# Linear attention and two MLPs: k and v on 128 partitions, earlier output operands, longer attention distances in the plan

## The chip, the cores and the metric

One NeuronCore of a Trainium2 chip runs the whole program. The metric is the device time of one execution in microseconds, given as the median of three runs. TensorE is PE in the profile, VectorE is DVE, ScalarE is ACT, GpSimd is POOL, and SP is the queue that issues nearly every DMA.

## The reference

The sizes: q, k and v are [8, 8, 576, 64] (batch, head, token, feature), and the result of attention, written as rows x[4608, 512], goes through two MLPs.

```python
q_s = exp(q - max(q, -1));  q_s = q_s / (sum(q_s, -1) + 1e-9)
k_s = exp(k - max(k, 2));   k_s = k_s / (sum(k_s, 2) + 1e-9)   # over the 576 tokens
kv = einsum('bhsd,bhse->bhde', k_s, v)
x = einsum('bhsd,bhde->bhse', q_s, kv)      # then rows (b, s), columns (h, d)
r = maximum(x @ w_in, 0);  x = (r * r) @ w_out              # w_in 512x2048
g = x @ w_gate;  out = (g * sigmoid(g) * (x @ w_val)) @ w_out2   # w_gate 512x1536
```

## The kernel before

Each float32 matmul is done as three products of a high part and a low part (`mm3`); `split` and `parts` make the parts with a cast on ACT and a subtraction on DVE. The 4608 rows are 9 blocks of 512. Blocks 0 to 2 go through the first MLP directly. Blocks 3 to 8 go through it as three pairs, and all blocks go through the second MLP as pairs, in seven products of quarter matrices instead of eight (`four`, `quarters`; the products come in the order "1", "5", "6", "2", "7", "3", "4").

**The order of the work.** The first block, to about 120 us, is an order written out by hand (`FIRST_BLOCK`). From there to the end of the gated half of the second MLP's first pair, `Plan.run` writes the order of every engine: it is a list scheduler that knows no times but those given in the source. Each unit is a generator whose `step` names an engine, a duration, what it needs, which buffers it takes and frees, and `land` and `wait`: with `wait=True` the unit's next step starts no earlier than the end plus `land`. Of the steps of one engine that could start within 0.3 us, the one with the lowest rank goes first. A step behind one of another engine is placed 1.7 us after its end where that was PE (0.4 us in the main stream of matmuls), 1.0 us where it was SP, and 0.2 us after the others. After the plan, Python's own order holds for SP, and the other engines are ordered by the framework.

**Attention in the plan.** `kv_unit` does two heads (`hp`): it loads k (`load_k`), starts `v_unit` (`load_v`), takes the maximum over tokens on DVE, transposes it on PE, reduces it on DVE, spreads it by a second transpose, subtracts on DVE, exponentiates on ACT, and `kv_sums` multiplies with v and a column of ones on PE. Tokens lie on 96 partitions with 6 tokens each, so a sum is 6 chunks for two heads. There are 32 such units: 4 at the start and 4 later in the hand-made order (`kv_steps`), 24 in the plan, 13 to 20 us apart.

**Operands of the first MLP's second product.** `out_part` has 24 operands besides those of product "1"; each is a `chunk`: a cast on ACT (L1182) and a subtraction on DVE (L1184) into one of 4 `uo` buffers. They have rank 1. At ranks below are `p5` (0.1) and `post` (0.2), which take results out of PSUM (L1242, L1258, L1272), and `sums` (0.5).

**The next x.** `second_x(1)` holds the operands of blocks 2 and 3 for the second MLP. Its first half is loaded by `after.load(0)` (four DMAs, L972) when the plan has ended; `between()` in `out_stage` splits it (L101, L102) between the products of the first pair's output.

Of the kernel before, what the change touches and what calls it, by code (L numbers as in the profile page):

```python
# [8 lines left out]
F32 = mybir.dt.float32  # L9
# [3 lines left out]
ALU = mybir.AluOpType  # L13
# [4 lines left out]
P = 128  # L18
# [4 lines left out]
def tile_linear_attention_two_mlps(  # L23
# [252 lines left out]
    def step(engine, d, needs=(), take=(), free=(), names=(), land=0.0, wait=False):  # L276
        return engine, d, needs, take, free, names, land, wait
# [286 lines left out]
    vt1 = att.tile([CK, 800], F32, name="vt")[:, 0:2 * NC * (D + 1)]  # L564
    vt1 = vt1.rearrange("p (h c d) -> p h c d", h=2, c=NC)
    kts, qs, qT, xT = {}, {}, {}, {}

    def load_k(b, hp, t=None):
        if t is None:
            t = kp.tile([CK, 2, NC, D], F32, name="kt", tag="kt")  # L570
        nc.sync.dma_start(t, k[b, 2 * hp:2 * hp + 2].rearrange("h (p c) d -> p h c d", c=NC))
        return t

    def load_v(b, hp, t=None):
        if t is None:
            t = vt1
        for h in range(2):
            nc.sync.dma_start(
                t[:, h, :, 0:D], v[b, 2 * hp + h].rearrange("(p c) d -> p c d", c=NC)
            )  # L580
        return t

    def load_kv(b, hp):
        kt = vt = None
        if hp % 2:
            kt, vt = (
                raws.tile([P, T], w_in.dtype, name="wraw", tag=f"raw{n}").bitcast(F32) for n in range(2)
            )
            kt = kt[:CK, 0:2 * NC * D].rearrange("p (h c d) -> p h c d", h=2, c=NC)
            vt = vt[:CK, 0:2 * NC * (D + 1)].rearrange("p (h c d) -> p h c d", h=2, c=NC)  # L590
            nc.gpsimd.memset(vt[:, :, :, D:D + 1], 1.0)
        kts[b, hp] = load_k(b, hp, kt), load_v(b, hp, vt)

# [45 lines left out]

    def kv_unit(j, i, hp):  # L640
        me = ("kv", j)
        yield step("SP", 0.5, [("kt.", j - 1)] + ([("x", 1, 3)] if j == 1 else []), [("kt", j)], (), [("kt.", j)], LAND_A, True)
        kt = None
        if hp % 2:
            kt = qtp.tile([P, 2, T], F32, name="kt", tag="qT1").rearrange("p a n -> p (a n)")
            kt = kt[:CK, 0:2 * NC * D].rearrange("p (h c d) -> p h c d", h=2, c=NC)
        kt = load_k(i, hp, kt)
        plan.unit(v_unit(j, i, hp), 2)
        yield step("DVE", 0.66)
        m3 = sp.tile([CK, 2, NC // 2, D], F32, name="m3", tag="m3", bufs=1)  # L650
        m1 = sp.tile([CK, 2, D], F32, name="m1", tag="m1")
# [3 lines left out]
        nc.vector.tensor_tensor(m1, m1, m3[:, :, 2], op=ALU.max)  # L655
# [5 lines left out]
        nc.vector.tensor_reduce(mx, pt[:, 0:CK], axis=AX.X, op=ALU.max)  # L661
        yield step("PE", 0.17)
        top = pt[:CK, P:2 * P]
        nc.tensor.transpose(top, mx.to_broadcast([P, CK]), ident)
        yield step("DVE", 0.95, (), (), [("pa", me)])
        nc.vector.tensor_tensor(
            kt, kt,
            top.rearrange("p (h d) -> p h d", h=2).unsqueeze(2).to_broadcast([CK, 2, NC, D]),
            op=ALU.subtract,
        )  # L670
        yield step("ACT", 0.84)
        nc.scalar.activation(kt, kt, AF.Exp)
        me = ("pk", j)
        yield step("PE", 1.0, [("vt.", j)], [("pa", me)], [("kt", j), ("vt", j)])
# [14 lines left out]

    def v_unit(j, i, hp):  # L690
        yield step("SP", 1.0, (), [("vt", j)], (), [("vt.", j)], LAND_A)
        load_v(i, hp)

    def q_unit(j, i, hp):
# [494 lines left out]
    def out_part(k, p, half, ops):  # L1189
# [294 lines left out]
    with tc.manual_schedule(engines={mybir.EngineType.SP}):  # L1484
# [41 lines left out]
        def kv_steps(b, hp):  # L1526
            if b:
                load_kv(b, hp)
                yield
            kt, vt = kts.pop((b, hp))  # L1530
            m3 = sp.tile([CK, 2, NC // 2, D], F32, name="m3", tag="m3", bufs=1)
            m = sp.tile([CK, 2, D], F32, name="m1", tag="m1")
            nc.vector.tensor_tensor(m3, kt[:, :, 0:3], kt[:, :, 3:6], op=ALU.max)
            yield
            nc.vector.tensor_tensor(m, m3[:, :, 0], m3[:, :, 1], op=ALU.max)
            yield
            nc.vector.tensor_tensor(m, m, m3[:, :, 2], op=ALU.max)
            yield
            pt = ps_a.tile([P, T], F32, name="pa", tag="pa")
            nc.tensor.transpose(pt[:, 0:CK], m.rearrange("p h d -> p (h d)"), ident[:CK, :CK])  # L1540
            yield
            mx = col.tile([P, 1], F32, name="mx", tag="mx")
            nc.vector.tensor_reduce(mx, pt[:, 0:CK], axis=AX.X, op=ALU.max)
            yield
            top = pt[:CK, P:2 * P]
            nc.tensor.transpose(top, mx.to_broadcast([P, CK]), ident)
            yield
            nc.vector.tensor_tensor(
                kt, kt,
                top.rearrange("p (h d) -> p h d", h=2).unsqueeze(2).to_broadcast([CK, 2, NC, D]),  # L1550
                op=ALU.subtract,
            )
            yield
# [172 lines left out]
        with tc.manual_schedule(engines=engines):  # L1726
# [102 lines left out]
```

## Time and profile before

| | us |
|---|---|
| median of 3 runs (1642.78 to 1643.26) | 1642.86 |
| the profiled execution | 1641.65 |
| its span, first to last instruction | 1639.8 |
| PE busy | 1602.0 |
| DVE busy | 1153.8 |
| ACT busy | 920.1 |

The span is the trace's; 1.85 us of the execution lie around it. An engine's busy time counts its instructions, overlapped ones once; what is left of the span is idle.

### The profile page before, as it was taken

Reading aid. Unit: us, or ns where it says so; the run is one execution under the profiler, and the core shown is the slowest. Engines: PE = TensorE matmul, PEld = TensorE weight load, DVE = VectorE, ACT = ScalarE, POOL = GpSimd, SP = SyncE. Lnnn points to the kernel's source line nnn. Section 1 sums busy time; section 2 is a strip of 40 time slices with the busy share of each in tenths; the row PEclk is TensorE's granted clock in tenths of the full one; section 3 lists DMA queues with packets and bytes.
Section 4 is the critical chain, followed back from the end, with each engine's and each line's share of the span. In section 5 each row is a group of like instructions: output and inputs, shape, how many; then the busy total and the mean of one; then the engine's idle time right before and its main releaser. Section 6 shows DMA issues by size and latency. Waiting matters only on the chain.

```text
span 1639.8 us, 23959 instructions
## 1 busy us (share of the span) xinstructions
PE 1602.0 (98%) x8114; PEld 1323.4 (81%) x8114; DVE 1153.8 (70%) x1857; ACT 920.1 (56%) x1561; POOL 376.9 (23%) x368
## 2 busy tenths in 40 slices
PE   7999999999999999999999999999999999999998
PEld 4777777878878888788878878888888888888898
DVE  8876776668978786888687778345844585447646
ACT  7775656668676776686755445334633463335334
POOL 4874554212221313021211200022001110210020
PEclk9999999999999999999999999999999999999999
DMA  9967999979998999899988987767686768667897
GB/s 300 282 208 235 306 307 302 300 237 291 270 283 255 290 327 330 302 348 322 349 288 298 307 293 235 231 192 219 219 243 193 220 210 253 194 204 210 264 385 257
DMA packets 280202, 440.97 MB, mean 269 GB/s; under 512 B 126864, under 2 KB 167824, under 8 KB 280080
## 3 DMA queue, kind: packets, MB, share of 16 engines
q1 hardware_dynamic: 279536, 439.30, 83.9%
q8 instruction: 65, 1.06, 0.3%
q14 instruction: 57, 0.47, 0.1%
q10 hardware_dynamic: 544, 0.13, 0.0%
HBM read 342.36 MB, written 96.99 MB: 268 GB/s over the span
## 4 chain that ended last, share of the span: by engine, by line
PE 81%; DVE 5%; DMA 5%; SPq 1%; ACT 1%; issue 1%; POOL 0%; DVEq 0%; POOLq 0%; ACTq 0%
PE ps L107 71%; PE acc L107 4%; PE ph L107 4%; DMA kt<-in_k_dram 2%; PE pa L617 1%; PE pa L107 1%; DVE uo L1184 1%; PE pa L734 1%; DMA w1d_out<-wbits 1%; DMA x<-x2d 0%; DVE st L1242 0%; DMA qs<-in_q_dram 0%; DVE u L1170 0%; DVE u L1168 0%; SPq L320 0%
## 5 line engine op out<-in xcount | busy, mean ns | idle before, releaser
L107 PE MATMUL ps<-w,wu 128*128 128x512 f32 (+1 forms) x3444 | 738.2, 375 | 1.2 <-ACT w L291 0.9
L107 PEld LDWEIGHTS ps<-w,wu 128*128 128x128 f32 x3444 | 610.3, 188 | 117.1 <-ACT w L291 1.4
L107 PE MATMUL ps<-uo,wu 128*128 128x512 f32 (+1 forms) x2172 | 475.5, 379 | 4.5 <-DVE uo L1184 2.7
L107 PEld LDWEIGHTS ps<-uo,wu 128*128 128x128 f32 x2172 | 390.2, 189 | 83.3 <-DVE uo L1184 5.5
L328 POOL TENSOR_TENSOR wsum<-wsum 128x256 f32<-128x256 f32 x124 | 112.4, 907 | 292.6 <-DVE wsum L404 130.9
L101 ACT CAST uo<-u 128x512 fp32r<-128x512 f32 (+1 forms) x204 | 116.4, 577 | 105.3 <-PE ps L107 42.6
L1436 POOL TENSOR_TENSOR u<-u 128x512 f32<-128x512 f32 (+1 forms) x24 | 27.6, 1152 | 577.6 <-DVE u L1432 577.6
L1431 DVE TENSOR_TENSOR u<-u,ps 128x512 f32<-128x512 f32 (+1 forms) x48 | 29.7, 620 | 174.5 <-ACT u L1430 174.5
L107 PE MATMUL ph<-xT,w 128*128 128x512 f32 x576 | 148.8, 399 | 2.1 <-ACT xT L771 0.7
L102 DVE TENSOR_TENSOR uo<-u,uo 128x512 fp32r<-128x512 f32 (+1 forms) x204 | 127.9, 645 | 31.0 <-ACT uo L101 30.7
L107 PE MATMUL acc<-g,w 128*128 128x512 f32 x576 | 145.0, 396 | 0.8 <-DVE g L1657 0.8
L1184 DVE TENSOR_TENSOR uo<-u,uo 128x512 fp32r<-128x512 f32 x168 | 116.4, 719 | 25.3 <-ACT uo L1182 25.1
L107 PEld LDWEIGHTS ph<-xT,w 128*128 128x128 f32 x576 | 105.1, 188 | 26.6 <-ACT xT L291 1.0
L107 PEld LDWEIGHTS acc<-g,w 128*128 128x128 f32 x576 | 105.6, 188 | 24.5 <-DVE g L1657 1.2
L1386 ACT COPY ps<-ps 128x512 f32<-128x512 f32 x102 | 58.1, 570 | 114.6 <-PE ps L107 113.4
L1182 ACT CAST uo<-u 128x512 fp32r<-128x512 f32 x168 | 100.0, 620 | 35.3 <-PE ps L107 34.3
L293 DVE TENSOR_TENSOR wst<-wsum,wst 128x512 fp32r<-128x512 f32 (+1 forms) x80 | 61.4, 770 | 21.2 <-ACT wst L291 18.9
L1086 ACT COPY ps<-ps 128x1024 f32<-128x1024 f32 x48 | 47.9, 998 | 50.0 <-PE ps L107 37.5
L714 POOL TENSOR_TENSOR qs<-qs,qr 128x512 f32<-128x512 f32 x28 | 32.1, 1147 | 124.9 <-DVE qr L712 94.1
L291 ACT CAST wst<-wsum 128x512 fp32r<-128x512 f32 (+1 forms) x80 | 46.8, 587 | 24.7 <-DVE wsum L404 12.0
L1138 ACT ACTIVATE u<-u 128x1024 f32<-128x1024 f32 x48 | 50.9, 1061 | 1.5
L293 DVE TENSOR_TENSOR g<-r,g 128x512 fp32r<-128x512 f32 x32 | 23.6, 739 | 38.9 <-ACT g L291 35.9
(216 smaller groups left out, 1891.5 us busy)
## 6 DMA issues: line engine op xcount, KB each, us to landing
wu<-gvd SPq DMA_DIRECT2D x210, 512.0 KB, 4.5
wu<-od SPq DMA_DIRECT2D x105, 512.0 KB, 4.4
wu<-hd SPq DMA_DIRECT2D x77, 512.0 KB, 6.1
wu<-ad SPq DMA_DIRECT2D x76, 512.0 KB, 5.2
gvd<-wst SPq DMA_DIRECT2D x72, 256.0 KB, 5.4
w<-in_moe_w_in_dram SPq DMA_DIRECT2D x16, 512.0 KB, 6.7
w<-in_moe_w_out_dram SPq DMA_DIRECT2D x16, 512.0 KB, 6.5
hd<-wst SPq DMA_DIRECT2D x32, 256.0 KB, 3.8
```

The lines of the kernel that those rows point to most:

```text
L101: nc.scalar.copy(hi, src)
L102: (eng or nc.vector).tensor_tensor(lo, src, f32(hi), op=ALU.subtract)
L107: nc.tensor.matmul(ps, lhsT=w[s], rhs=x[t], start=start and n == 0, stop=stop and n == 2, skip_group_check=more,)
L291: nc.scalar.copy(hi, src)
L293: nc.vector.tensor_tensor(lo, src, f32(hi), op=ALU.subtract)
L328: nc.gpsimd.tensor_tensor(to, x, y, op=op)
L714: nc.gpsimd.tensor_tensor(t, t, r.unsqueeze(3).to_broadcast([P, TJ, 2, D]), op=ALU.mult)
L1086: nc.scalar.copy(open_bank(k, to), source)
L1138: nc.scalar.activation(u, u, AF.Square)
L1182: nc.scalar.copy(t[:, 0], src())
L1184: nc.vector.tensor_tensor(t[:, 1], src(), f32(t[:, 0]), op=ALU.subtract)
L1386: nc.scalar.copy(x, y)
```

## The change

- k and v: tokens on 128 partitions, 5 chunks (`NC`) instead of 6. Partitions 0 to 63 hold 5 tokens each, 64 to 127 hold 4 tokens in chunks 1 to 4. Chunk 0 of the upper half of k is filled with a row that stands elsewhere too (rows of five overlap by one), which changes no maximum, and `kv_sums` reads 64 partitions alone for that chunk. A load of k becomes two DMAs, one of v four instead of two. The planner's costs follow: 1.0 instead of 0.5 on SP for k, 1.5 instead of 1.0 for v.
- attention's distances: three DVE steps of `kv_unit` ahead of a PE step have 0.8 us of `land` with `wait`, the exponential has 0.6.
- the rank of the 24 output operands is 0.05 instead of 1.
- the next x: its first half is loaded by a step of the plan, once four of six gated parts are done, instead of behind the plan.

```diff
-    CK = 96
-    NC = S // CK
+    NC, HALF = 5, P // 2
...
     def load_k(b, hp, t=None):
         if t is None:
-            t = kp.tile([CK, 2, NC, D], F32, name="kt", tag="kt")
-        nc.sync.dma_start(t, k[b, 2 * hp:2 * hp + 2].rearrange("h (p c) d -> p h c d", c=NC))
+            t = kp.tile([P, 2, NC, D], F32, name="kt", tag="kt")
+        rows = k[b, 2 * hp:2 * hp + 2]
+        low = rows[:, 0:HALF * NC].rearrange("h (p c) d -> p h c d", c=NC)
+        nc.sync.dma_start(t[0:HALF], low)
+        high = rows[:, HALF * NC - 1:S - 1].rearrange("h (p c) d -> p h c d", c=NC - 1)
+        high = bass.AP(tensor=high.tensor, offset=high.offset, ap=[*high.ap[:2], (D, NC), (1, D)])
+        nc.sync.dma_start(t[HALF:P], high)
         return t
...
         for h in range(2):
-            nc.sync.dma_start(
-                t[:, h, :, 0:D], v[b, 2 * hp + h].rearrange("(p c) d -> p c d", c=NC)
-            )
+            rows = v[b, 2 * hp + h]
+            low = rows[0:HALF * NC].rearrange("(p c) d -> p c d", c=NC)
+            nc.sync.dma_start(t[0:HALF, h, :, 0:D], low)
+            high = rows[HALF * NC:S].rearrange("(p c) d -> p c d", c=NC - 1)
+            nc.sync.dma_start(t[HALF:P, h, 1:NC, 0:D], high)
...
     def kv_sums(pk, kt, vt):
         for c in range(NC):
+            n = P if c else HALF
             for j in range(2):
                 nc.tensor.matmul(
-                    pk[j * D:(j + 1) * D, 0:D + 1], lhsT=kt[:, j, c, :], rhs=vt[:, j, c, :],
+                    pk[j * D:(j + 1) * D, 0:D + 1], lhsT=kt[0:n, j, c, :], rhs=vt[0:n, j, c, :],
...
-        yield step("DVE", 0.66)
+        yield step("DVE", 0.5)
...
-        nc.vector.tensor_tensor(m3, kt[:, :, 0:3], kt[:, :, 3:6], op=ALU.max)
-        yield step("DVE", 0.82)
+        nc.vector.tensor_tensor(m3, kt[:, :, 0:2], kt[:, :, 2:4], op=ALU.max)
+        yield step("DVE", 0.82, land=0.8, wait=True)
...
-        nc.tensor.transpose(pt[:, 0:CK], m1.rearrange("p h d -> p (h d)"), ident[:CK, :CK])
-        yield step("DVE", 0.25)
+        nc.tensor.transpose(pt[:, 0:P], m1.rearrange("p h d -> p (h d)"), ident)
+        yield step("DVE", 0.25, land=0.8, wait=True)
...
-        yield step("ACT", 0.84)
+        yield step("ACT", 0.73, land=0.6, wait=True)
...
-                plan.unit(chunk(p, half, 4 * x + f, lambda us=us, w=where[name], j=j: us[w][:, j], needs, free), 1)
+                plan.unit(chunk(p, half, 4 * x + f, lambda us=us, w=where[name], j=j: us[w][:, j], needs, free), 0.05)
...
+            ahead = second_x(1)
+
+            def load_ahead():
+                yield step("SP", 2.0, [("gated", NG - 3)], (), (), ["ahead"])
+                ahead.load(0)
+
+            plan.unit(load_ahead(), 1)
             plan.run(
-                [("gated", f) for f in range(NG)] + [("wu", stream.n_pairs + 7 * NG + 3)]
+                ["ahead"] + [("gated", f) for f in range(NG)] + [("wu", stream.n_pairs + 7 * NG + 3)]
...
             if g == 0:
-                ops = first
-                after = second_x(g + 1)
-                after.load(0)
+                ops, after = first, ahead
```

The first block's `kv_steps` change in the same way.

## Rows read from the trace of the kernel before

**Rows 1.** The page's first part: busy time, share of the span, instructions.

```profile
span 1639.8 us, 23959 instructions
PE 1602.0 (98%) x8114; PEld 1323.4 (81%) x8114; DVE 1153.8 (70%) x1857; ACT 920.1 (56%) x1561; POOL 376.9 (23%) x368
```

**Rows 2.** Windows by stage: length, busy time per engine, granted clock, DMA share, GB/s.

```profile
0.00:20.00 20.00, 9.35 (x67) 6.11 (x68) 14.91 (x36) 12.66 (x46) 7.16 (x22) 1.00 1.06 250
...
120.00:512.00 392.00, 380.96 (x2255) 308.01 (x2254) 287.41 (x512) 260.74 (x448) 136.27 (x135) 1.00 0.92 277
512.00:860.00 348.00, 342.69 (x1505) 280.15 (x1506) 280.63 (x380) 235.83 (x344) 63.08 (x59) 1.00 0.91 316
...
984.00:1540.00 556.00, 556.00 (x2455) 460.36 (x2454) 335.57 (x521) 237.13 (x406) 71.01 (x54) 1.00 0.72 217
1540.00:1639.80 99.80, 95.17 (x776) 94.22 (x774) 51.59 (x120) 38.21 (x87) 13.43 (x18) 0.99 0.90 321
```

**Rows 3.** PE's waits, 120 to 980: line, whom it waited for, sum, times, longest.

```profile
PE ps L107 <- DVE uo L1184: 4.1, 5, 1.5
PE pa L664 <- DVE mx L661: 2.1, 4, 1.5
PE pa L658 <- DVE m L655: 1.6, 2, 0.8
PE pa L617 <- ACT kt L672: 1.4, 2, 1.1
PE ps L107 <- ACT uo L101: 1.1, 1, 1.1
...
PE ps L107 <- DVE uo L102: 0.7, 1, 0.7
```

**Rows 4.** Groups by line and shape on PE: attention's matmuls in the plan.

```profile
L617 PE MATMUL pa<-vt,kt 96*64 96x65 f32 x624 | 24.2, 225 | 2.6 <-ACT kt L672 1.4 <-ACT e L723 0.7 <-DMA vt<-in_v_dram 0.3
...
L664 PE MATMUL pa<-ident,mx 128*96 128x128 f32 x24 | 6.7, 279 | 2.1 <-DVE mx L661 2.1
L658 PE MATMUL pa<-ident,m 96*128 96x96 f32 x24 | 6.2, 258 | 2.7 <-DVE m L655 1.6 <-DVE qT L293 1.0
```

**Rows 5.** Timeline, 283 to 286: start, length, instruction, idle time before.

```profile
285.12 0.92 PE L617 MATMUL pa<-vt,kt 96*64 96x65 f32 x24 [1.06 <-ACT kt L672]
...
285.98 0.50 PE L107 MATMUL ph<-xT,w 128*128 128x512 f32 x1
```

**Rows 6.** Lines 571, 578 and 117: DMA issues on SP (min/median/max ns), landing.

```profile
L571 SPq DMA_DIRECT2D kt<-in_k_dram x26: 334/436/2292, 30.7 to 467.1; - x26
...
L578 SPq DMA_DIRECT2D vt<-in_v_dram x52: 574/587/1404, 31.1 to 479.9; - x52
...
DMA to landing us min/median/max: 4.1/6.5/11.8
```

**Rows 7.** Timeline, 0 to 26: the first weight load and its first reader.

```profile
12.47 1.60 SPq L117 DMA_DIRECT2D w<-in_moe_w_in_dram  x2
...
19.88 0.63 ACT L150 ACTIVATE acc<-w 128x512 f32<-128x512 f32 x1
```

**Rows 8.** Timeline, 664 to 672: the longest wait for an output operand.

```profile
668.51 2.35 DVE L1242 TENSOR_TENSOR st<-st,ps 128x1024 f32<-128x1024 f32 x2 [0.29 <-PE ps L107]
...
670.78 1.89 DVE L1184 TENSOR_TENSOR uo<-u,uo 128x512 fp32r<-128x512 f32 x3
671.52 0.73 PE L107 MATMUL ps<-uo,kv 128*128 128x512 f32 x2 [1.46 <-DVE uo L1184]
```

**Rows 9.** Timeline, 950 to 1000: the next x is loaded and split.

```profile
966.34 1.85 SPq L972 DMA_DIRECT2D x<-x2d  x4
...
974.33 0.62 ACT L101 CAST w<-x 128x512 fp32r<-128x512 f32 x1 [3.40 <-DMA x<-x2d]
```

**Rows 10.** Windows around that place, columns as in rows 2.

```profile
976.00:980.00 4.00, 2.17 (x9) 1.27 (x8) 4.00 (x7) 3.10 (x6) 0.00 (x0) 0.98 1.03 420
980.00:983.00 3.00, 3.00 (x8) 2.35 (x8) 3.00 (x6) 3.00 (x7) 0.00 (x0) 0.50 1.03 411
```

More of the change, by code (lines that the diff above doesn't have):

```diff
@@ L563, in tile_linear_attention_two_mlps @@
     kf = att.tile([P, P], F32, name="kf")
-    vt1 = att.tile([CK, 800], F32, name="vt")[:, 0:2 * NC * (D + 1)]
+    vt1 = att.tile([P, 800], F32, name="vt")[:, 0:2 * NC * (D + 1)]
     vt1 = vt1.rearrange("p (h c d) -> p h c d", h=2, c=NC)
@@ L588, in load_kv @@
             )
-            kt = kt[:CK, 0:2 * NC * D].rearrange("p (h c d) -> p h c d", h=2, c=NC)
-            vt = vt[:CK, 0:2 * NC * (D + 1)].rearrange("p (h c d) -> p h c d", h=2, c=NC)
+            kt = kt[:, 0:2 * NC * D].rearrange("p (h c d) -> p h c d", h=2, c=NC)
+            vt = vt[:, 0:2 * NC * (D + 1)].rearrange("p (h c d) -> p h c d", h=2, c=NC)
             nc.gpsimd.memset(vt[:, :, :, D:D + 1], 1.0)
@@ L641, in kv_unit @@
         me = ("kv", j)
-        yield step("SP", 0.5, [("kt.", j - 1)] + ([("x", 1, 3)] if j == 1 else []), [("kt", j)], (), [("kt.", j)], LAND_A, True)
+        yield step("SP", 1.0, [("kt.", j - 1)] + ([("x", 1, 3)] if j == 1 else []), [("kt", j)], (), [("kt.", j)], LAND_A, True)
         kt = None
@@ L645, in kv_unit @@
             kt = qtp.tile([P, 2, T], F32, name="kt", tag="qT1").rearrange("p a n -> p (a n)")
-            kt = kt[:CK, 0:2 * NC * D].rearrange("p (h c d) -> p h c d", h=2, c=NC)
+            kt = kt[:, 0:2 * NC * D].rearrange("p (h c d) -> p h c d", h=2, c=NC)
         kt = load_k(i, hp, kt)
         plan.unit(v_unit(j, i, hp), 2)
-        yield step("DVE", 0.66)
-        m3 = sp.tile([CK, 2, NC // 2, D], F32, name="m3", tag="m3", bufs=1)
-        m1 = sp.tile([CK, 2, D], F32, name="m1", tag="m1")
@@ L652, in kv_unit @@
-        nc.vector.tensor_tensor(m3, kt[:, :, 0:3], kt[:, :, 3:6], op=ALU.max)
-        yield step("DVE", 0.82)
+        yield step("DVE", 0.5)
+        m3 = sp.tile([P, 2, 2, D], F32, name="m3", tag="m3", bufs=1)
+        m1 = sp.tile([P, 2, D], F32, name="m1", tag="m1")
+        nc.vector.tensor_tensor(m3, kt[:, :, 0:2], kt[:, :, 2:4], op=ALU.max)
+        yield step("DVE", 0.82, land=0.8, wait=True)
         nc.vector.tensor_tensor(m1, m3[:, :, 0], m3[:, :, 1], op=ALU.max)
-        nc.vector.tensor_tensor(m1, m1, m3[:, :, 2], op=ALU.max)
+        nc.vector.tensor_tensor(m1, m1, kt[:, :, 4], op=ALU.max)
@@ L656, in kv_unit @@
         yield step("PE", 0.17, (), [("pa", me)])
         pt = pa_tile()
-        nc.tensor.transpose(pt[:, 0:CK], m1.rearrange("p h d -> p (h d)"), ident[:CK, :CK])
-        yield step("DVE", 0.25)
+        nc.tensor.transpose(pt[:, 0:P], m1.rearrange("p h d -> p (h d)"), ident)
+        yield step("DVE", 0.25, land=0.8, wait=True)
         mx = col.tile([P, 1], F32, name="mx", tag="mx")
-        nc.vector.tensor_reduce(mx, pt[:, 0:CK], axis=AX.X, op=ALU.max)
+        nc.vector.tensor_reduce(mx, pt[:, 0:P], axis=AX.X, op=ALU.max)
@@ L662, in kv_unit @@
         yield step("PE", 0.17)
-        top = pt[:CK, P:2 * P]
-        nc.tensor.transpose(top, mx.to_broadcast([P, CK]), ident)
-        yield step("DVE", 0.95, (), (), [("pa", me)])
+        top = pt[:, P:2 * P]
+        nc.tensor.transpose(top, mx.to_broadcast([P, P]), ident)
+        yield step("DVE", 0.84, (), (), [("pa", me)])
         nc.vector.tensor_tensor(
             kt, kt,
-            top.rearrange("p (h d) -> p h d", h=2).unsqueeze(2).to_broadcast([CK, 2, NC, D]),
+            top.rearrange("p (h d) -> p h d", h=2).unsqueeze(2).to_broadcast([P, 2, NC, D]),
@@ L669, in kv_unit @@
             op=ALU.subtract,
         )
-        yield step("ACT", 0.84)
+        yield step("ACT", 0.73, land=0.6, wait=True)
         nc.scalar.activation(kt, kt, AF.Exp)
         me = ("pk", j)
-        yield step("PE", 1.0, [("vt.", j)], [("pa", me)], [("kt", j), ("vt", j)])
+        yield step("PE", 0.85, [("vt.", j)], [("pa", me)], [("kt", j), ("vt", j)])
         pk = pa_tile()
@@ L690, in v_unit @@
     def v_unit(j, i, hp):
-        yield step("SP", 1.0, (), [("vt", j)], (), [("vt.", j)], LAND_A)
+        yield step("SP", 1.5, (), [("vt", j)], (), [("vt.", j)], LAND_A)
         load_v(i, hp)
@@ L1495, in tile_linear_attention_two_mlps @@
         for hp in range(NP):
-            kt = borrowed()[:CK, 0:2 * NC * D].rearrange("p (h c d) -> p h c d", h=2, c=NC)
-            vt = borrowed()[:CK, 0:2 * NC * (D + 1)].rearrange("p (h c d) -> p h c d", h=2, c=NC)
+            kt = borrowed()[:, 0:2 * NC * D].rearrange("p (h c d) -> p h c d", h=2, c=NC)
+            vt = borrowed()[:, 0:2 * NC * (D + 1)].rearrange("p (h c d) -> p h c d", h=2, c=NC)
             nc.gpsimd.memset(vt[:, :, :, D:D + 1], 1.0)
@@ L1530, in kv_steps @@
             kt, vt = kts.pop((b, hp))
-            m3 = sp.tile([CK, 2, NC // 2, D], F32, name="m3", tag="m3", bufs=1)
-            m = sp.tile([CK, 2, D], F32, name="m1", tag="m1")
-            nc.vector.tensor_tensor(m3, kt[:, :, 0:3], kt[:, :, 3:6], op=ALU.max)
+            m3 = sp.tile([P, 2, 2, D], F32, name="m3", tag="m3", bufs=1)
+            m = sp.tile([P, 2, D], F32, name="m1", tag="m1")
+            nc.vector.tensor_tensor(m3, kt[:, :, 0:2], kt[:, :, 2:4], op=ALU.max)
             yield
@@ L1536, in kv_steps @@
             yield
-            nc.vector.tensor_tensor(m, m, m3[:, :, 2], op=ALU.max)
+            nc.vector.tensor_tensor(m, m, kt[:, :, 4], op=ALU.max)
             yield
             pt = ps_a.tile([P, T], F32, name="pa", tag="pa")
-            nc.tensor.transpose(pt[:, 0:CK], m.rearrange("p h d -> p (h d)"), ident[:CK, :CK])
+            nc.tensor.transpose(pt[:, 0:P], m.rearrange("p h d -> p (h d)"), ident)
             yield
             mx = col.tile([P, 1], F32, name="mx", tag="mx")
-            nc.vector.tensor_reduce(mx, pt[:, 0:CK], axis=AX.X, op=ALU.max)
+            nc.vector.tensor_reduce(mx, pt[:, 0:P], axis=AX.X, op=ALU.max)
             yield
-            top = pt[:CK, P:2 * P]
-            nc.tensor.transpose(top, mx.to_broadcast([P, CK]), ident)
+            top = pt[:, P:2 * P]
+            nc.tensor.transpose(top, mx.to_broadcast([P, P]), ident)
             yield
@@ L1549, in kv_steps @@
                 kt, kt,
-                top.rearrange("p (h d) -> p h d", h=2).unsqueeze(2).to_broadcast([CK, 2, NC, D]),
+                top.rearrange("p (h d) -> p h d", h=2).unsqueeze(2).to_broadcast([P, 2, NC, D]),
                 op=ALU.subtract,
```

## The prediction

> **What bounds the kernel now.** The page's first part comes first: PE is busy for 1602.0 of 1639.8 us, DVE for 1153.8, ACT for 920.1 [rows 1]. So only two things can pay: less work on PE, or less of its 37.8 idle us. The windows by stage say where those are [rows 2]: 10.65 at the start, 11.04 from 120 to 512 (attention in the plan), 5.31 from 512 to 860 (the pairs of the first MLP), nothing from 984 to 1540, and 4.63 in the last stage. The list of PE's waits then names who is late between 120 and 980 [rows 3]: output operands, attention's k chain, and the hand-over from the plan to the next x. The change goes to these three. Lastly the timeline is read at each place.
>
> The sum is made against the profiled execution, 1641.65 us, which is 1.2 under the median of the runs (1642.86); the predicted time is moved up by that 1.2.
>
> **k and v on 128 partitions: PE.** There are 32 sums; 28 of them lie in stretches where PE is nearly always busy (24 planned, 4 in the later hand-made order), and 4 at the start. The 624 records of the planned group are 26 sums of 24 records, and the union of 24.2 us gives 0.93 us each [rows 4]; the timeline shows one at 0.92 [rows 5]. One chunk of six by proportion is 0.153. But the last record's 0.22 us is paid once: (0.92 - 0.22) / 11 steps between 12 pairs of records is 0.064, and a chunk is two steps, 0.127. I take 0.127, the cautious end: 28 x 0.127 = 3.6 us less. The first transpose now moves 128 columns, as the second does: 279 against 258 ns [rows 4], 28 x 0.021 = 0.6 us more.
>
> The new sum changes from 64 to 128 rows between its first and second chunk, and no row shows that. The nearest one is the change from the 96-row sum to a 128-row matmul, which starts at 285.98, before the sum has ended at 286.04 [rows 5]: nothing is lost there. The upper bound is that the second chunk waits for the first one's full 0.22 us [rows 4], 28 x 0.22 = 6.2 us. I take 0.05 each, near the row that shows no gap, 1.4 us. Net: 3.6 - 0.6 - 1.4 = 1.6 us less, between 3.7 less (0.153 and no loss at the change of rows) and 3.2 more.
>
> The Trainium skill speaks against this part: TensorEngine Tiling (Array Packing), Key Properties, says that a change of tiling mode drains TensorE. This case's rows 5 show no gap where the rows change from 96 to 128; with a full drain the net would be the 3.2 us more.
>
> **k and v: DVE and ACT.** The maximum takes 256 instead of 384 elements, the subtraction and the exponential 640 instead of 768. That is some tenths of a us per unit on engines that are 70% and 56% busy [rows 1]. PE's matmuls of other units cover it, so I count nothing; without the cover it would be a gain.
>
> **k and v: SP and the transfers.** A k load becomes two issues, each between 0.33 (the shortest k issue) and 0.44 us: 0.2 to 0.5 us more. A v load becomes four with about half the pieces each, between 0.33 and 0.59 us: 0.1 to 1.2 more [rows 6]. I take 0.4 and 0.6, so 1.0 us of SP per unit, which is what the planner's costs grow by. Queued behind them on SP are weight loads, other attention loads and stores. In the plan I count nothing: the units are at least 13 us apart, and the longer distances cover a k that lands a little later. If that cover is gone, it is the slower rival below.
>
> At the start the order is fixed and SP issues 12 more DMAs ahead of the first weight load. That load is issued at 12.47 and its first reader on ACT starts at 19.88 [rows 7]; a median landing of 6.5 us [rows 6] puts its landing at 19.0, so 0.9 us is spare. DMA is full there, with a share of 1.06 at 250 GB/s [rows 2], so the queue is held by transfers as well as by issuing. The bounds: if the 12 issues add 0.38 each, 4.6 us less the spare 0.9 is 3.7 us later; if transfers set the pace, 4 x 32 KB more of k at 250 GB/s are 0.5 us, inside the spare. The shorter DVE and ACT work there could give 0.5 back. I take 0.5 us more, near the end that the full DMA share speaks for.
>
> **Output operands ahead.** PE waits five times for L1184, 4.1 us [rows 3]. At the longest, DVE does two result additions (L1242, 2.35 us) and only then the three operands [rows 8]. With rank 0.05 the operand goes ahead of `p5` and `post`; a `p5` that is 0.7 us later has the products "6" and "2" as cover, two times four chunks of 1.36 us by the plan's figures, before its bank is needed for product "7". An instruction of 1.2 us that already runs can't be overtaken, so I take three quarters: 3.0 us less, between 1 and 4.1. What could be late next is the result addition, whose cover was just given.
>
> **Longer distances.** PE's waits for m1 (L658 for L655), the reduced maximum (L664 for L661) and the exponential (L617 for L672) are 1.6 + 2.1 + 1.4 = 5.1 us in eight waits, the longest 1.5 [rows 3]. With 0.8 us more distance (0.6 for the exponential) the two long ones keep 0.7 and 0.5, so up to 3.9 go. A unit gets 2.2 us longer, within its 13 us. As all of the plan's order moves, I take half: 2.0 us less, between 0 and 3.9.
>
> **The next x earlier.** The four loads are issued at 966.34 and ACT waits 3.40 us for one of them at 974.33 [rows 9]. The casts and subtractions of the output operands stand behind these splits, and PE waits 1.1 + 0.7 us for them [rows 3], inside 976 to 980 [rows 10]. Then the granted clock is 0.50 from 980 to 983, the lower level of 1.2 GHz, straight after TensorE had idled 1.83 of 4 us [rows 10]; half of 3 us and 0.02 of 4 us are 1.6 us more. So the place costs 3.4 us. Moved ahead, the four issues take their 1.85 us of SP between weight loads of the gated parts, which are loaded five slots ahead, and the x lands long before the plan ends. But DVE was busy 4.00 of the 4.00 us [rows 10], so part of the wait is DVE's queue and stays: I take half of the 1.8 and most of the clock's 1.6, together 2.5 us less, between 0.5 and 3.4.
>
> **The new order.** The planner writes everything from 120 us anew with other costs. The waits there that the change doesn't aim at (7 us or so of the 11.04 + 5.31) can come out shorter or longer; an order that the change was not made for seldom comes out all for the better, so 1.0 us more, between 3 less and 6 more.
>
> The sum: -1.6 + 0.5 - 3.0 - 2.0 - 2.5 + 1.0 = -7.6 us, so 1634.0 for a profiled execution and **1635.2 us** for the median.
>
> **Rivals.** *The order gives it back* (same). If the planned waits outside the change's aim grow by 6 rather than 1 us, 5 more than in the sum, the time is 1640.2, within 0.2% of before; for it speaks that PE's waits between 120 and 512 have many owners, none above 2.1 us [rows 3]; against it, that the gains at the output operands and at the next x don't hang on attention's order. The change would there do what it says and be eaten.
>
> *The sum drains at its change of rows* gives 6.2 instead of 1.4 us, 1640.0, the same side. Against it stands the start at 285.98 [rows 5].
>
> *All margins hold*: no loss by the new order or at the change of rows, 3.7 from PE, 3.9, 4.1 and 3.4 us from the three waits, nothing at the start, together 15.1 us less: 1627.8.
>
> *Slower: k lands beyond its margin.* Its place is the planned attention, 120 to 512, where the DMA share is 0.92 [rows 2]. PE's transposes and sums stand in one queue with the MLP's matmuls, so each k that comes later than planned stops them. A k is now two transfers of 160 KB each, issued one after the other, with four of v behind it instead of two. If each of the 24 planned units is late by 0.7 us beyond the 0.8 us added, that costs 16.8 us against the 7.6 gained: 1652.0. It decides from 0.32 us per unit on (7.6 / 24). For it speaks the DMA share; against it the small excess of bytes, 32 KB on 288, 0.1 us at 277 GB/s, and that SP's step is planned 0.5 us longer.
>
> The Trainium skill has a rule for this rival: DMA: Bandwidth & Descriptors, Rules for kernel authors, says that two transfers to disjoint partition halves serialize, and advises one transfer over all 128 partitions. It agrees with a full DMA in rows 2, but no row before shows such halves; by the rule the second half's landing is the one that counts, which is the rival's mechanism.
>
> **How the numbers follow.** Forecast 0.52, all margins hold 0.14, given back or drained 0.20, slower 0.14. A measurement here tells about 0.2% (3.3 us) from no change. Faster by more than that, under 1639.6: forecast and all margins, 0.66. Within: 0.20. Slower, above 1646.1: 0.14. The likeliest case's own range is 1631 to 1639. The 8 in 10 range leaves out a little of the best case and most of the slower one: 1627 to 1646.
>
> **What the profile after would show.** Groups of 20 instead of 24 records per sum, at 0.80 us each, would show the first step right; 0.9 or more would show the drain. PE's waits for L1184 below 1.5 us, the three k waits below 3 us, the first weight's reader within 0.5 us of 19.88, no idle place on PE around 977 and no granted clock of 0.50 there would show the others. The prediction is wrong if new waits between 120 and 980 outgrow the three removed, or if the reader of the first weight comes 2 us or more later.

## The result, and the profile after

The change made the kernel slower: 1662.85 us median of 5 runs (1658.92 to 1664.0) against 1642.86 before (1639.29 to 1644.79), a ratio of 1.0121, 95% interval 1.0102 to 1.0139. The forecast was 1635.2, with a range of 1627 to 1646. The profiled execution has a span of 1660.8 us against 1639.8. From here on the stages are bounded by four events on PE in the profiled execution of each kernel: the end of the last first-product matmul of block 0, the first matmul of the pairs, the short matmul that closes the plan, and the end.

| us | block 0 done | to the pairs | to the plan's end | to the end | span |
|---|---|---|---|---|---|
| before | 120.5 | 232.5 | 615.8 | 671.1 | 1639.8 |
| after | 128.9 | 240.5 | 622.9 | 668.4 | 1660.8 |
| difference | +8.5 | +8.0 | +7.1 | -2.7 | +20.9 |

The page's first part and the windows of after, for [rows 1, 2]:

```profile
span 1660.8 us, 23883 instructions
PE 1612.9 (97%) x7986; PEld 1325.2 (80%) x7986; DVE 1145.2 (69%) x1857; ACT 916.8 (55%) x1561; POOL 379.9 (23%) x368
```

```profile
0.00:20.00 20.00, 7.84 (x55) 5.24 (x55) 11.18 (x29) 10.91 (x42) 4.81 (x20) 1.00 0.70 175
...
120.00:512.00 392.00, 375.85 (x2103) 299.13 (x2101) 265.55 (x495) 245.62 (x430) 137.98 (x136) 0.99 0.88 266
512.00:860.00 348.00, 342.32 (x1526) 280.20 (x1526) 276.04 (x373) 241.69 (x351) 65.49 (x59) 1.00 0.91 308
```

PE is idle 10.1 us more and busy 10.9 us more, though it has 128 matmuls fewer. In the first 20 us the DMA share fell from 1.06 to 0.70, in the planned attention from 0.92 to 0.88: the transfers did not become the limit, they were started later. Part of the busy time is the lower clock: three stretches of 3.4 us at a granted clock of 0.50 (1.2 GHz) that before does not have, up to 1.7 us each; before has one, at the hand-over [rows 10]. PE had stood idle 2.18 us ahead of the first and 3.25 us ahead of the second:

```profile
74.00:78.00 4.00, 4.00 (x13) 2.71 (x13) 2.60 (x4) 1.90 (x4) 0.50 (x2) 0.57 1.01 298
238.00:242.00 4.00, 4.00 (x28) 3.19 (x27) 3.40 (x9) 0.70 (x2) 1.06 (x1) 0.57 0.96 292
```

PE's waits from 120 to 1005, for [rows 3]:

```profile
PE pa L624 <- ACT kt L679: 5.2, 3, 3.2
PE ps L106 <- DVE u L1161: 4.1, 4, 1.4
PE pa L106 <- DVE qT L292: 2.3, 4, 0.8
...
PE pa L665 <- ACT kf L691: 1.9, 2, 1.1
PE pa L106 <- ACT kf L691: 1.8, 1, 1.8
PE ps L106 <- DVE uo L101: 1.1, 1, 1.1
```

Of the three waits that the distances aimed at, those for m1 and for the reduced maximum are at 0.2 and gone; the one for the exponential (L679, L672 before) grew from 1.4 to 5.2. With it stand other waits for ACT's late results. SP's issues of k and v, for [rows 6] (lower and upper half of k, then of v):

```profile
L572 SPq DMA_DIRECT2D kt<-in_k_dram x26: 606/612/1472, 35.6 to 492.4; - x26
...
L575 SPq DMA_DIRECT2D kt<-in_k_dram x26: 606/612/657, 36.3 to 493.3; - x26
...
L584 SPq DMA_DIRECT2D vt<-in_v_dram x52: 533/563/1652, 36.9 to 506.4; - x52
...
L586 SPq DMA_DIRECT2D vt<-in_v_dram x52: 533/615/1132, 37.6 to 507.0; - x52
```

A half costs SP about as much as a whole did, or more: 0.61 us each for k's two where the whole took 0.44, 0.56 and 0.61 us for v's where the whole took 0.59. A unit's medians go from 0.44 + 2 x 0.59 = 1.6 to 2 x 0.61 + 2 x (0.56 + 0.61) = 3.6 us, 2.0 us more.

The start, for [rows 7]:

```profile
17.67 0.61 SPq L584 DMA_DIRECT2D w<-in_v_dram  x1
18.33 0.61 SPq L586 DMA_DIRECT2D w<-in_v_dram  x1
18.98 1.16 SPq L116 DMA_DIRECT2D w<-in_moe_w_in_dram  x2
...
23.40 0.63 ACT L149 ACTIVATE acc<-w 128x512 f32<-128x512 f32 x1 [1.13 <-DMA w<-in_moe_w_in_dram]
```

SP issues k, q and v one behind the other up to there. The first weight load goes out 6.5 us later than at 12.47. Its reader starts 3.5 us later and now waits for it; before, the load had landed at 17.94, 1.9 us ahead of its reader. The sums and the first transpose, for [rows 4, 5]:

```profile
L624 PE MATMUL pa<-vt,kt 128*64 128x65 f32 x384 | 17.0, 230 | 0.0
L624 PE MATMUL pa<-vt,kt 64*64 64x65 f32 x96 | 8.6, 243 | 5.4 <-ACT kt L679 5.2 <-DMA vt<-in_v_dram 0.2
L665 PE MATMUL pa<-ident,m 128*128 128x128 f32 x24 | 6.8, 285 | 2.1 <-ACT kf L691 1.9 <-DVE m L662 0.2
```

```profile
439.38 0.95 PE L624 MATMUL pa<-vt,kt 64*64 64x65 f32 x20
```

A sum has 20 records instead of 24 and takes 0.95 us at the full clock, not less than the 0.92 of before.

At the hand-over the x is loaded at 961.59, 30 us ahead of the plan's end, and PE has no gap of 1.8 us there and no half clock, for [rows 9, 10]:

```profile
961.59 2.15 SPq L979 DMA_DIRECT2D x<-x2d  x4
```

```profile
990.00:994.00 4.00, 4.00 (x19) 3.14 (x18) 3.87 (x7) 1.85 (x4) 0.00 (x0) 1.00 0.49 141
994.00:998.00 4.00, 4.00 (x19) 3.30 (x18) 4.00 (x8) 1.77 (x4) 0.00 (x0) 1.00 0.95 355
998.00:1002.00 4.00, 3.34 (x15) 2.44 (x13) 4.00 (x8) 0.93 (x3) 0.00 (x0) 1.00 1.03 421
```

**One wait followed back.** At 234.57 to 237.82 PE stands 3.25 us for an exponential. The timeline:

```profile
231.00 0.56 SPq L584 DMA_DIRECT2D vt<-in_v_dram  x1
231.60 0.61 SPq L586 DMA_DIRECT2D vt<-in_v_dram  x1
232.31 1.02 SPq L319 DMA_DIRECT2D ad<-wst  x2
...
234.25 0.81 DVE L673 TENSOR_TENSOR kt<-kt,pa 128x640 f32<-128x640 f32 x1
...
235.99 0.62 ACT L290 CAST wst<-wsum 128x512 fp32r<-128x512 f32 x1 [4.47 <-DMA ad<-wst]
236.52 0.62 ACT L713 ACTIVATE qs<-qs 128x512 f32<-128x512 f32 x1
237.05 0.72 ACT L679 ACTIVATE kt<-kt 128x640 f32<-128x640 f32 x1
...
237.82 0.99 PE L624 MATMUL pa<-vt,kt 64*64 64x65 f32 x16 [3.25 <-ACT kt L679]
```

The exponential's own input is ready at 235.06. In ACT's order a cast stands ahead of it into `wst`, a buffer in which quarter matrices are staged for a store to DRAM. The cast waits 4.47 us until the buffer's earlier stores have landed (issued at 232.31, the last lands at 235.89). On SP those stores stood behind four issues for q, one for x and four for v, which run one behind the other from 226.38 on. The wait is named after ACT, but a late issue on SP made it. Over 120 to 350, ACT's waits for these stores are:

```profile
ACT wst L290 <- DMA ad<-wst: 18.0, 7, 4.5
...
ACT wst L290 <- DMA hd<-wst: 1.1, 1, 1.1
```

That is 19.1 us. Before, in the same view:

```profile
ACT wst L291 <- DMA ad<-wst: 4.4, 4, 1.5
```

### The profile page after: what moved, and what is told of

It is laid out like the page before. It is cut to its first block, busy times and chain, and to the rows that moved or that the text cites. A ratio compares the mean times of both kernels' runs of the same rounds, so it can differ in the third digit from the quotient of the medians.

```text
span 1660.8 us, 23883 instructions
## 1 busy us (share of the span) xinstructions
PE 1612.9 (97%) x7986; PEld 1325.2 (80%) x7986; DVE 1145.2 (69%) x1857; ACT 916.8 (55%) x1561; POOL 379.9 (23%) x368
## 4 chain that ended last, share of the span: by engine, by line
PE 74%; DMA 6%; DVE 5%; ACT 3%; SPq 3%; issue 2%; POOL 1%; DVEq 0%; ACTq 0%; POOLq 0%
PE ps L106 65%; PE ph L106 3%; PE acc L106 3%; DMA kt<-in_k_dram 1%; PE pa L106 1%; DMA qs<-in_q_dram 1%; DMA ad<-wst 1%; PE pa L624 1%; DMA od<-o 1%; SPq L319 1%; PE pa L741 1%; DVE u L1161 1%; DVE u L1327 0%; DMA wu<-hd 0%; SPq L586 0%
## 5 line engine op out<-in xcount | busy, mean ns | idle before, releaser
L292 DVE TENSOR_TENSOR wst<-wsum,wst 128x512 fp32r<-128x512 f32 (+1 forms) x80 | 57.1, 716 | 18.6 <-ACT wst L290 18.3
L292 DVE TENSOR_TENSOR g<-r,g 128x512 fp32r<-128x512 f32 x32 | 27.9, 873 | 35.6 <-ACT g L290 35.5
L711 POOL TENSOR_TENSOR qs<-qs,qm 128x512 f32<-128x512 f32 x28 | 33.4, 1194 | 81.0 <-DVE qm L709 55.3
```

Of the source, the lines that this page charges most:

```text
L292: nc.vector.tensor_tensor(lo, src, f32(hi), op=ALU.subtract)
L711: nc.gpsimd.tensor_tensor(t, t, m.unsqueeze(3).to_broadcast([P, TJ, 2, D]), op=ALU.add)
```

## The experiments

The first theory was that SP's queue, lengthened by more issues, delays everything behind it. The rivals: the planner's new order loses time as such; the halves cost through their transfers, whoever issues them; the sum's change of rows costs PE time. All results in one table. The stages are those above; "stores" is ACT's waits for the stores of `wst` and "k" DVE's waits for loads of k, both from 120 to 350; "issuing" is the sum of SP's issue durations in that stretch of 230 us. All but the ratios in us. Medians and ratios are of all executions, each ratio to the kernel before on the same chip in the same session; the other columns are read from one profiled execution each. That of halves was its fastest, 1659.48 us, so its stages are no upper end.

| run | median | ratio (95%) | block 0 | to pairs | to plan's end | to end | stores | k | issuing |
|---|---|---|---|---|---|---|---|---|---|
| before | 1642.86 | 1 | 120.5 | 232.5 | 615.8 | 671.1 | 4.4 | 10.8 | 165.3 |
| after | 1662.85 | 1.0121 (1.0102-1.0139) | 128.9 | 240.5 | 622.9 | 668.4 | 19.1 | 11.0 | 186.3 |
| others | 1647.28 | 1.0036 (1.0022-1.0050) | 120.2 | 235.5 | 621.5 | 668.3 | 13.0 | 18.5 | 171.2 |
| only128 | 1674.62 | 1.0196 (1.0167-1.0224) | 128.7 | 243.9 | 623.8 | 676.9 | 11.8 | 10.2 | 184.5 |
| halves | 1665.15 | 1.0139 (1.0102-1.0176) | 124.8 | 247.7 | 616.6 | 668.6 | 15.1 | 15.6 | 184.4 |
| halves_head | 1645.93 | 1.0037 (1.0021-1.0052) | 123.3 | 233.9 | 615.2 | 669.5 | 3.9 | 8.2 | 161.8 |
| rows64 | 1643.92 | 1.0022 (1.0007-1.0037) | 121.9 | 232.9 | 615.6 | 669.3 | 0.5 | 6.7 | 162.5 |
| rank | 1640.99 | 1.0003 (0.9991-1.0015) | 120.4 | 232.3 | 618.4 | 667.1 | 3.6 | 9.2 | 162.8 |
| dist | 1657.86 | 1.0113 (1.0098-1.0128) | 121.0 | 237.0 | 619.2 | 677.4 | 17.8 | 16.3 | 168.2 |
| ahead | 1642.74 | 1.0008 (0.9995-1.0020) | 120.6 | 234.1 | 614.9 | 671.9 | 3.5 | 7.6 | 160.5 |
| dist_ahead | 1656.95 | 1.0088 (1.0070-1.0106) | 120.3 | 234.8 | 623.9 | 676.4 | 15.7 | 17.8 | 166.3 |
| same_order | 1667.12 | 1.0153 (1.0133-1.0173) | 129.3 | 252.5 | 615.7 | 668.7 | 21.7 | 18.0 | 187.6 |
| full_rows | 1661.62 | 1.0120 (1.0102-1.0137) | 126.9 | 240.9 | 622.5 | 668.3 | 26.4 | 14.1 | 187.9 |
| pool_half | 1646.21 | 1.0026 (1.0013-1.0039) | 129.9 | 229.0 | 618.1 | 668.5 | 3.9 | 1.1 | 156.8 |
| hybrid | 1638.72 | 0.9985 (0.9972-0.9998) | 122.5 | 228.3 | 619.6 | 668.4 | 9.4 | 5.4 | 164.2 |
| hybrid_sp | 1654.89 | 1.0089 (1.0075-1.0103) | 121.0 | 243.3 | 620.5 | 668.3 | 14.8 | 12.8 | 189.6 |
| hybrid_layout | 1663.54 | 1.0141 (1.0126-1.0157) | 122.8 | 237.2 | 624.8 | 677.2 | 1.7 | 4.6 | 161.4 |

The six kernels with three more issues per planned unit on SP (after, only128, halves, same_order, full_rows, hybrid_sp) issue for 184 to 190 us and need 240 to 253 to the pairs; the other eleven issue for 157 to 171 and need 228 to 237. The waits for stores alone do not decide it: dist has 17.8 us of them and needs 237.0.

The next stage divides the kernels in another way. The six kernels whose planner inputs are the old ones, or differ in the load of the next x alone (before, halves, halves_head, rows64, same_order, ahead), need 614.9 to 616.6 us to the plan's end, whether SP issues more or not; the eleven with other inputs need 618.1 to 624.8. So the 7.1 us that after loses there go with the new order and not with SP's issues; hybrid and hybrid_sp differ by 0.9 there.

**The change in two parts: others, only128.** The kernel before with the rank, the distances and the early x (their hunks of the diff), and the kernel with the layout and its planner costs alone.

> The kernel before with the three other edits alone (rank of the output operands, attention's distances, the next x in the plan), k and v on 96 partitions. Theory A (the 128-partition layout, its loads and its change of rows, costs the 20 us): some 5 to 8 us under before, 1635 to 1638. Theory B (the planner's new order costs it): 1650 or more.

> The kernel before with k and v on 128 partitions and the planner's costs for it, without the three other edits. Theory A: 1660 to 1668, with the first weight load issued near 19 us instead of 12.5. Theory B: within 8 us of before, 1643 to 1651.

Both lose, and neither theory has the times: others lies between its two values, only128 beyond 1668. The layout loses 8.2 us at the start and 11.4 to the pairs, and 13.8 more behind. The other three lose 3.0 and 5.7 us and give back 2.8 at the end.

**More issues alone: halves.** Layout, bytes, arithmetic and the planner's order stay as before; only the loads are cut in two.

```diff
-        nc.sync.dma_start(t, k[b, ...].rearrange("h (p c) d -> p h c d", c=NC))
+        for p in (slice(0, CK // 2), slice(CK // 2, CK)):
+            nc.sync.dma_start(t[p], k[b, ...].rearrange("h (p c) d -> p h c d", c=NC)[p])
...
+            for p in (slice(0, CK // 2), slice(CK // 2, CK)):
+                nc.sync.dma_start(t[p, h, :, 0:D], v[b, 2 * hp + h].rearrange(...)[p])
```

> The kernel before with each load of k and v cut into two of 48 partitions, same bytes, same pieces, same planned order. If it is the number of DMA issues that costs (Theory A1): an issue of 0.5 us or more each, the first weight load issued 5 us later or more, and 1650 to 1660 in all. If the pieces' form on 128 partitions costs (A2): issues near half the time each, and under 1647.

This alone costs 4.3 us at the start and 15.2 to the pairs, as much as the whole change, with no new order and no change of rows. The median is 5 us beyond the range expected. A half of k takes 0.43 us to issue and a half of v 0.60, about what the wholes take, so A2 falls; k's halves stay under the 0.5 of A1.

**The start alone: halves_head.** The same cut where `b == 0`, the first four units.

> Only the loads of the first four pairs of heads cut into two of 48 partitions, all else as before. If the queue's issues bound the start: the first weight load issued 3 us later or more and 3 to 5 us in all (1643 to 1646). If the loss of the halved loads lies in the plan: within 1 us of before.

The first weight load goes out at 17.51, 5.0 us later, and block 0 ends 2.9 us later; the ratio is 1.0037. Most of what halves lost lies in the plan.

**The change of rows alone: rows64.** The first of six chunks reads 64 of 96 rows, so the output leaves out a third of that chunk's tokens.

```diff
+            n = CK if c else 64
-                    ... lhsT=kt[:, j, c, :], rhs=vt[:, j, c, :],
+                    ... lhsT=kt[0:n, j, c, :], rhs=vt[0:n, j, c, :],
```

> The kernel before whose sums read 64 of 96 partitions in the first of six chunks, so the output leaves out a third of that chunk's tokens; loads and order as before. If a change of rows drains PE: each sum 1.1 us instead of 0.93, 28 x 0.15 = 4 us at most, 1644 to 1648. If it costs nothing: 1642 to 1644 and a sum of 0.93 us.

```profile
464.07 1.06 PE L618 MATMUL pa<-vt,kt 64*64 64x65 f32 x24
```

The same 24 records take 1.06 us instead of 0.92: a change of rows inside a sum costs 0.14 us. The ratio of 1.0022 (1.0007 to 1.0037) is some 3.6 us, near the 3.9 of 28 such sums, though the profiled execution, the fastest of ten, is not longer than that of before.

**One edit each: rank, dist, ahead.** The hunks of the diff one by one, on the kernel before.

> The kernel before with the rank of the 24 output operands at 0.05 and nothing else. As the prediction had it: 3 us faster, waits for L1184 gone. Rival, from the trace with all three edits (waits for L1154 of 4.1 us in place of those for L1184): within 1.5 us of before, the wait only moves.

> The kernel before with attention's longer distances alone. As the prediction had it: 2 us faster. Rival (the order written anew loses more than the margin saves): 3 to 7 us slower, lost between 120 and 360.

> The kernel before with the next x loaded in the plan and nothing else. If the wait and the half clock at the hand-over were due to the late load: 2.5 to 3.5 us faster, and no granted clock of 0.50 behind it. If DVE's queue keeps the wait: within 1 us.

Rank makes no difference that can be measured. The waits for L1184 went from 4.1 to 0.6, but a new one is there, for the operand taken out of PSUM ahead of it:

```profile
PE ps L107 <- DVE u L1154: 2.7, 3, 1.4
...
PE ps L107 <- ACT w L291: 1.9, 2, 0.9
...
PE ps L107 <- DVE uo L1184: 0.6, 1, 0.6
```

The distances alone lose 1.1%, some 18 us, where the rival had 3 to 7: 4.5 us to the pairs, 3.4 to the plan's end, 6.3 behind it, where late weight loads and output operands stop PE:

```profile
PE ps L107 <- DVE uo L1184: 4.8, 8, 1.5
PE ps L107 <- DMA wu<-od: 3.6, 1, 3.6
PE pa L658 <- DVE m L655: 3.4, 2, 3.0
```

The wait for m1, which the distances aimed at, grew from 1.6 to 3.4. Loading x early makes no difference alone, and the half clock behind the hand-over is still there, at 981.9.

**Is it the early x that mends the hand-over? dist_ahead.**

> The kernel before with two of the four edits: the longer distances and the next x loaded in the plan. The distances alone gave 1657.9, of which 6.2 us were lost after the plan, where the loads of the next x stood between late weight loads. If the early load repairs that place, 1649 to 1653 and PE's waits for DMA near 983 gone; if it is the order of the weight loads alone that is late there, 1656 to 1659.

No. The last stage stays at 676.4, with a longer wait for the same weight load:

```profile
PE ps L107 <- DMA wu<-od: 5.6, 1, 5.6
```

With the rank as well (others) it is 668.3: with the longer distances, the rank mends that place. All seven kernels with the rank have 667.1 to 668.5 there, the ten without it 668.6 to 677.4. But halves, halves_head, rows64 and same_order, with neither rank nor early load, have 668.6 to 669.5 and no half clock at the hand-over. And of the 66 executions of the kernel before beside the experiments, 20 show a mean granted clock of 1.000, so no such stretch. The place is not slow in every execution; the early load was not seen to mend it.

**The layout in the old order: same_order.** Planner costs, distances, rank and x as before.

> The 128-partition layout of k and v with its six issues per unit, while the planner keeps the costs, distances, ranks and the place of the next x that it has in the kernel before. First theory (more issues on SP's queue make the transfers late): the cutting of the loads alone cost 19.5 us up to the first product of the pairs, so this one should lose 15 to 22 us by then, with 27 to 30 us instead of 24.7 at the first matmul of a block, and end at 1657 to 1667. Rival (the planner's new costs write a worse order): with the old order the loss shrinks to the start's 3 to 5 us and the sums' change of rows, 1643 to 1650.

1667.12, just beyond the first theory's range, and 28.8 us lost up to the pairs where it gave 15 to 22. The rival falls up to the pairs: with the old costs that stage is 12 us longer than in after. Behind the pairs it holds: only128 differs from same_order in the planner's costs alone; the new costs gain 8.6 us to the pairs and lose 16.3 behind, in ratios 1.0196 against 1.0153.

**No change of rows: full_rows.** The changed kernel with all sums over 128 rows.

```diff
+        nc.gpsimd.memset(vt1[HALF:P, :, 0, :], 0.0)      # and once in each borrowed v
-            n = P if c else HALF
+            n = P
```

> The changed kernel with chunk 0 of v's upper half set to zero by GpSimd once per buffer, and all sums over 128 rows, so that no sum changes its number of rows. Theory of the drain (the change from 64 to 128 rows costs 0.15 us in a sum and its 28 sums 4 us): sums of 0.80 to 0.85 us instead of 0.99, and 1658 to 1660 in place of 1662.8. Rival (the time between the records is what the modelled ends make of it, or other waits take it): 1661 to 1664, sums still above 0.93 us.

```profile
L625 PE MATMUL pa<-vt,kt 128*64 128x65 f32 x480 | 20.0, 227 | 2.8 <-ACT kt L680 2.5 <-DMA vt<-in_v_dram 0.2
```

20.0 us for 24 sums are 0.83 each, so the drain was there and is gone; but the time is that of after within its interval. The first theory had the sums and the rival the time. PE's own work was not what its planned part waited for.

**The upper halves on another queue: pool_half.**

```diff
-        nc.sync.dma_start(t[HALF:P], high)
+        nc.gpsimd.dma_start(t[HALF:P], high)
...
-            nc.sync.dma_start(t[HALF:P, h, 1:NC, 0:D], high)
+            nc.gpsimd.dma_start(t[HALF:P, h, 1:NC, 0:D], high)
```

> The changed kernel with the upper half of every load of k and v (three of six issues per unit) issued from GpSimd's queue instead of SP's; the order is that of the changed kernel. First theory (SP's queue): SP's issues per unit go back to three, the first weight load goes out at 13 to 15 us instead of 18.98, and the pairs start 8 to 14 us earlier than at 369.5, so 1648 to 1655; less is gained if GpSimd's own queue stands behind waits of its own. Rival (the order, or the transfers themselves, whoever issues them): within 3 us of 1662.8.

1646.2, better than was expected, but still above the kernel before (1.0026, 1.0013 to 1.0039): the stage to the pairs falls from 240.5 to 229.0, 3.5 less than before the change. Block 0 stays late (129.9), though the first weight load goes out at 12.66: there PE waits 2.3 us for POOL's part of g, and POOL has three more issues per unit to do.

**Nothing but the queue: hybrid, hybrid_sp.** The hand-ordered units keep 96 partitions and whole loads; the planned ones have the new layout and sums over 128 rows. The two kernels differ only in the engine that issues the upper halves.

```diff
-        nc.gpsimd.dma_start(t[HALF:P], high)
+        nc.sync.dma_start(t[HALF:P], high)
...
-            nc.gpsimd.dma_start(t[HALF:P, h, 1:NC, 0:D], high)
+            nc.sync.dma_start(t[HALF:P, h, 1:NC, 0:D], high)
```

> The changed kernel with three things moved: the eight hand-ordered units keep 96 partitions and their three issues each; the 24 planned units have 128 partitions with the upper halves issued from GpSimd's queue; and planned sums read 128 rows in all five chunks (v's unused quarter set to zero once). Theory of SP's issues: block 0 ends at 120.5 as in the kernel before, the planned part to the first product of the pairs takes the 229.0 us that it took with GpSimd's issues or less, the rest some 1288 us as there: 1637 to 1641, faster than before. Rival (the layout or the other edits lose of themselves): 1643 to 1650.

> The same with all six issues of a planned unit on SP's queue; nothing else differs from the kernel with GpSimd's issues, neither the start nor the order nor the sums. Theory of SP's issues: 24 units with 3 issues of 0.6 us more each, where SP is already busy with issuing for seven tenths of the time: 7 to 14 us slower than the one with GpSimd's queue. Rival (the halves cost through the transfers, whoever issues them): within 3 us of it.

```profile
226.04 0.80 PE L648 MATMUL pa<-vt,kt 128*64 128x65 f32 x20 [0.31 <-ACT kt L703]
```

That is one sum of hybrid. 1638.72 against 1654.89: three more issues per planned unit on SP cost 16.2 us, more than the 7 to 14 expected. In the two profiled executions the stage to the pairs is 15.0 longer. The windows of that stretch, hybrid and then hybrid_sp:

```profile
120.00:350.00 230.00, 224.43 (x1312) 180.15 (x1309) 153.31 (x294) 140.75 (x264) 122.73 (x147) 1.00 0.93 280
```

```profile
120.00:350.00 230.00, 215.03 (x1207) 171.30 (x1206) 139.85 (x272) 131.72 (x246) 90.06 (x95) 0.98 0.86 266
```

The same bytes: issued from two queues they fill the DMA to 0.93 and PE to 224.4 us, from one to 0.86 and 215.0. The price of the other queue is 29.0 us of POOL, which counts as busy with these issues and has that time free there:

```profile
L610 POOL DMA_DIRECT2D vt<-in_v_dram x31 | 19.3, 629 | 24.0 <-PE pa L648 18.6 <-PE pa L695 5.4
...
L595 POOL DMA_DIRECT2D kt<-in_k_dram x16 | 9.7, 604 | 0.0
```

This pair leaves two rivals. The profile lists POOL's transfers as another kind (software_dynamic, in larger packets), so they might be cheaper; but POOL's upper halves of k land 5.1 us after their issue in the median and those of SP in hybrid_sp 3.5, which does not look cheaper. And a second queue could help because SP never has more than 8 transfers outstanding in any trace of this case. But counted from issue to landing between 120 and 350, SP is at 8 for 18.2 us in hybrid_sp and for 47.1 in hybrid: the slower kernel meets that limit less.

Hybrid is also the one version that comes out faster than the kernel before, by 0.15% (0.02 to 0.28): an interval that only just leaves out no change, for one of sixteen versions.

**The other edits with the queue relieved: hybrid_layout.** Hybrid without rank, distances and early x.

> The one with GpSimd's issues, without the rank, the distances and the early load of the next x: the layout alone, with the planner's new costs. If the three other edits pay once SP's queue is not lengthened: 2 to 6 us slower than with them. If they are neutral or lose, as they did on the kernel before (1.0036): the same or faster, with the hand-over's half-clock place back.

Expected were 2 to 6 us; it is 25 us slower than hybrid: 8.9 us to the pairs, 5.2 to the plan's end, 8.8 behind, with the half clock at the hand-over back. Two of these edits were worth nothing on the kernel before and the third lost 1.1%. What an edit of the plan's costs is worth hangs on the order that the list scheduler makes of all of them; it doesn't add up.

## Why the prediction was wrong

**SP in the plan is the step that failed:** "In the plan I count nothing: the units are at least 13 us apart, and the longer distances cover a k that lands a little later." I asked whether k would be late and not how full the queue was, and put the cost at nothing. SP issued for 165.3 of 230 us before; with 2.0 us more per unit (I had 1.0) it issues for 186.3, 81% of the time, and what falls behind are the stores and loads that stand after k and v. Hybrid and hybrid_sp put 16.2 us on this alone. A second term was too small: the new order, below.

**The slower rival** had the right place and the wrong mechanism. Between 120 and 350, k's transfers land 3.4 us after their issue in the median, against 4.6 for the whole loads before, DVE waits for them 11.0 us against 10.8, and PE hardly waits for what DVE makes of them. The upper half, issued 0.66 us behind the lower, lands 0.62 us behind it in the median of 26 pairs. The Trainium skill's rule that such halves serialize (DMA: Bandwidth & Descriptors, Rules for kernel authors) can't be tested by these landings: 160 KB take 0.6 us at the 266 GB/s of that stretch, about as long as the second issue is behind the first. Its advice to use one transfer over all partitions holds here all the same, for the issuing. The same page (Issuing engines are not separate DMA queues) says that several issuing engines save only the sequencer's time, "usually small relative to the DMA itself". The runs agree that this time is what the second engine saved. One by one it is small, 0.61 us against 3.4, but the queue adds these up, and by hybrid_sp it is what holds this stage.

**The start**, predicted at +0.5 with a bound of 3.7: the reader of the first weight is 3.5 later, at the bound, but the first matmul of block 0 is 5.5 and its end 8.5 later, 1.7 of it half clock. A reader 2 us or more later was one of the prediction's own signs of being wrong. I took the DMA share of 1.06 for the limit; in after SP issues without a pause and the share is 0.70. The twelve issues cost 6.5 us of SP, 0.54 each, not 0.38. Of the 8.5 us at the end of block 0, halves_head gives 2.9 to more issues; the rest is not traced to a cause.

**PE's sums**: the term was right in kind and mis-sized at the change of rows, 0.05 taken and about 0.15 measured (0.95 less the 0.80 that a sum of hybrid takes). A sum got 0.03 longer and the transpose 0.027, so 28 of each are 1.6 us more, where 1.6 less was forecast. The Trainium skill's drain (TensorEngine Tiling (Array Packing), Key Properties) agrees with this loss at a change within a sum, about two thirds of one record's 0.22 us; [rows 5] had shown another kind of change.

**Output operands**, -3.0: the waits for L1184 went and came back as 4.1 us for the operand's source, evicted from PSUM by the same DVE (L1161). I had named the result addition as the next to be late; it was this eviction. **Longer distances**, -2.0: the edit lengthens two DVE steps, not three, and the exponential. The m1 and maximum waits fell to 0.2 in after, the exponential's grew to 5.2, so the three did not fall below 3; alone the edit loses 1.1%. **The next x**, -2.5: the last stage did gain 2.7, but the early load alone is worth nothing measurable, the rank alone gains 4.0 there, and the half clock that the 1.6 us stood for is not in every execution of before. **The new order**, +1.0 with 6 as a bound: the stage to the plan's end alone lost 7.1, a stage in which all eleven new orders lose 2.3 to 9.0 and the old ones at most 0.8. With the distances alone both planned stages lost.

What stays open: how much of after's 20 us the four parts hold each, since they don't add up; what makes most of the first block's 8.5 us; why it stays 2 us late in hybrid; and what in the new orders costs the time behind the pairs.

## What to carry over

Where one queue issues nearly all transfers, count its issues as an engine's work: number times the measured issue time against the stretch, stores included; here, at 72%, three more per unit were no longer free. A wait named after a compute engine can be a store that was issued late: look at what stands ahead of the late instruction on its engine, and what that waits for. An edit to a list scheduler's costs can't be priced by the waits that it aims at; only the new order shows it.

## What was not expected of the hardware

- An issue on SP costs about the same for less data: 0.61 us for 160 KB of k on 64 partitions, 0.44 for 288 KB on 96, and 0.43 for each half of 48 in halves. The bytes don't set it; what does is open.
- TensorE loses 0.14 to 0.15 us when consecutive matmuls of a sum go from 64 to 96 or 128 rows, some 3.6 us for 28 sums on the kernel before (rows64); where late issues bound the stage, taking the losses away changed the time by nothing that could be measured (full_rows against after).
- The same loads issued from SP and POOL together moved 280 GB/s between 120 and 350, from SP alone 266.
- SP never had more than 8 transfers outstanding in any of the 17 traces.
